# Attention, MoE and soft MoE on one core: where the sums of the attention weights are inverted

## The chip, the cores and the metric

The kernel runs on one core of a Trainium2 chip. A core has a matrix engine (TensorE, PE; its weight loads are listed as PEld), a vector engine (VectorE, DVE), a scalar engine (ScalarE, ACT), GpSimd (POOL) and a queue that issues transfers (SyncE, SP). The metric is the time of one execution on the device, in microseconds, as the median of several runs.

## The reference

```python
scores = (1 / sqrt(64)) * q @ k.T            # 4 batches, 12 heads, 448 rows, head size 64
scores = where(upper triangle, -1e9, scores)
attn = exp(scores - max(scores, axis=-1))
attn = attn / (attn.sum(axis=-1) + 1e-9)
x = (attn @ v), heads side by side           # 1792 x 768
g = leaky_relu(x @ w_in); x = g @ w_out      # 768 -> 2048 -> 768
logits = x @ phi                             # 32 slots: 8 experts of 4
slots = softmax over rows(logits).T @ x      # each expert: relu(. @ w1[e]) @ w2[e]
out = softmax over slots(logits) @ slot_out  # 1792 x 768
```

What matters here is the fourth line: every row of `attn @ v` is divided by the sum of the exponentials of its row.

## The kernel before, in words

Attention works on 24 pairs of heads (pair n is pair n % 6 of batch n // 6), transposed: keys lie on partitions in blocks of 112, the 448 query rows on columns. Pair n takes three slots of work. In slot A `attend` multiplies the exponentials of pair n - 1 with v (tile `O`, both heads, 64 partitions each), `lowering` brings the negated row maxima of pair n to columns, the product S3 and the product T0 of scores follow. In slot B `inverses(n - 1)` makes the row sums, then come S02 and T1. In slot C `columns(n - 1)` normalises, then come T2, S1 and the transposes `qkps` of a later pair. S tiles feed the row maxima (`junk`, line 361, on VectorE), T tiles the exponentials (`P`, line 397, on ScalarE). S and T tiles share two PSUM buffers, the many small products two buffers named "tr".

GpSimd masks the diagonal blocks of `P` and adds the key blocks into `tsum`, so that a row sum is a sum over partitions of `tsum` (and, for the first 112 rows, of the first block of `P`); partitions 112 to 127 hold small constants that add the reference's epsilon.

`inverses` (line 427): the weights `sixteen[:, i]` have ones in 16 of 64 columns and zeros in the others. Four products per head, accumulated in one tile `dn` of 128x112, place the sum of row 112 i + c into partitions 16 i to 16 i + 15 of column c. One reciprocal on VectorE (line 438) inverts all. `columns` (line 440): eight products with `first`, which picks one partition of r, spread the inverses to `rb`, 128x448, so that all 64 partitions of a head hold the inverse of their column. ScalarE copies that to SBUF (`rs`, line 452), VectorE multiplies with `O` and a scale (line 458), ScalarE rounds to fp16 (line 459) and GpSimd forms the remainder (line 460).

Each matrix product of type fp32 is two instructions in the trace, so eight products are 16.

From the second batch on, each slot also holds one of the 16 up products H of the batch before: 18 products of fp16 pieces (line 596) into one PSUM buffer, read by ScalarE (`g`, line 614) and then VectorE (line 615); the next H waits for that. Two of 18 slots in each batch have no H. Beside it, w_in is converted from 64 bit numbers during pairs 6 to 11, w_out after that: `cv`, `cs`, `w_am`, `w_m` (lines 108 to 245) on ScalarE, VectorE and GpSimd, and `wt_ps`, `wp_ps`, `wf_ps` (small products of w_out and phi) on TensorE. After attention comes the last up product with transposes `gps`, logits `L` and slot sums `pg`, then the experts, fed by a stream of w1 and w2 (line 820), whose buffers come free as TensorE finishes with what lies in them.

The order on each engine is set by the framework's list scheduler, which walks the program with its own costs and takes attention and H ahead of the conversions. Products made by `mm` and `tr` keep their program order on TensorE.

Of the kernel before, what the change touches and what calls it, by code (L numbers as in the profile page):

```python
# [10 lines left out]
F32 = mybir.dt.float32  # L11
# [23 lines left out]
def tile_attn_moe_softmoe(ctx: ExitStack, tc: tile.TileContext, q, k, v, w_in, w_out, phi, w1, w2, out, dbg=None):  # L35
    nc = tc.nc
    dbg = dbg or {}

    B, H, S, D = q.shape
# [5 lines left out]
    CP = 112  # L45
    NI = S // CP
    NP = H // 2
# [31 lines left out]
    att = tc.alloc_tile_pool(name="att", bufs=1, side="right")  # L79
# [9 lines left out]
    def ps_tr(name, shape=(128, 512)):  # L89
        return psum.tile(list(shape), F32, tag="tr", bufs=TR[0], name=name)  # L90
# [12 lines left out]
    mm = partial(in_order, nc.tensor.matmul)  # L103
# [310 lines left out]
    r_t = {}  # L414
# [11 lines left out]

    def inverses(n):

        p = pbuf[n % 2]
        dn = ps_tr(f"dn{n}", (128, CP))  # L430
        for i in range(NI):
            for a in range(2):
                x = p[0][:, a, 0, :CP] if i == 0 else tsum[:, a, CP * (i - 1) : CP * i]
                mm(
                    dn[64 * a : 64 * a + 64], sixteen[:, i], x, start=i == 0, stop=i == NI - 1, skip_group_check=True,
                )
        r_t[n] = r = att.tile([128, CP], F32, tag="r", bufs=1, name=f"r{n}")
        nc.vector.reciprocal(r, dn)

    def columns(n):  # L440

        b, hp = divmod(n, NP)
        o, r = o_t.pop(n), r_t.pop(n)
        rb = ps_tr(f"rb{n}", (128, S))
        for i in range(NI):
            for a in range(2):
                mm(
                    rb[64 * a : 64 * a + 64, CP * i : CP * (i + 1)], first[:, i, a], r, start=True, stop=True,
                    skip_group_check=True,
                )  # L450
        rs = att.tile([128, S], F32, tag="rs", bufs=1, name=f"rs{n}")
        nc.scalar.copy(rs, rb)
        if hp == 0:
            x16[b] = xpool.tile([128, CHUNK // 2], F16, tag="x16", name=f"x16_{b}")[:, : NP * 2 * S].rearrange(
                "p (c x s) -> p c x s", c=NP, x=2
            )
        hi = x16[b][:, hp, 0]
        nc.vector.scalar_tensor_tensor(rs, o, s_v[b], rs, ALU.mult, ALU.mult)
        nc.scalar.copy(hi, rs)  # L459
        nc.gpsimd.tensor_tensor(x16[b][:, hp, 1], rs, hi, ALU.subtract)  # L460

    NPAIR = B * NP
    onesr = att.tile([128, CP], F32R, name="onesr")
# [8 lines left out]
    first = att.tile([128, NI, 2, 64], F32, name="first")  # L472
# [12 lines left out]
    tsum = att.tile([128, 2, S - CP], F32, name="tsum")  # L485
# [6 lines left out]
    def attention_slots():  # L492
# [10 lines left out]
        for n in range(NPAIR + 1):  # L503
# [10 lines left out]
            if n > 0:  # L514
                inverses(n - 1)
# [5 lines left out]
            if n > 0:  # L521
                columns(n - 1)
# [226 lines left out]
    if True:  # L749
# [105 lines left out]
        for c in range(4):  # L855
            wo = loaded.pop(("wo", c))
            for h in range(2):
                for t in range(4):
                    nc.tensor.matmul(
                        psi[h][32 * t : 32 * t + 32], gdt[:, t, c], wo[:, t, 384 * h : 384 * (h + 1)],  # L860
                        start=c == 0, stop=c == 3, skip_group_check=True,
# [17 lines left out]
        for e in range(E):  # L879
            ph = ps2(f"ph{e}", (128, 256), tag="h", bufs=4)  # L880
            for hf in range(2):
                wt = loaded.pop(("w1", (e, hf)))
                for t in range(3):
                    for g in range(4):
                        nc.tensor.matmul(  # L885
                            ph[32 * g : 32 * g + 32], sit[:, 3 * hf + t], wt[:, t, 256 * g : 256 * (g + 1)],
                            start=hf == 0 and t == 0, stop=hf == 1 and t == 2, skip_group_check=True,
# [69 lines left out]
        for x, (t0, nt, c0, cols) in enumerate(pieces):  # L957
# [4 lines left out]
            for h in (0, 1) if cols == DM else (c0 // DH,):  # L962
                for t in range(nt):
# [3 lines left out]
                        start=t0 + t < 4, stop=t0 + t >= 8 * E - 4, skip_group_check=True,  # L967
# [52 lines left out]
```

## Time and profile before

| | us |
|---|---|
| median of 3 runs (lowest, highest) | 733.87 (732.2, 735.56) |
| the profiled execution | 740.27 |
| its span | 738.5 |
| TensorE busy | 639.2 |
| VectorE busy | 344.6 |
| ScalarE busy | 305.9 |
| GpSimd busy | 228.9 |

The span is the time from the first to the last instruction of the profiled execution, and busy times are sums over all stretches of the program. Pairs 0 to 5 are normalised in the first 105 us; pairs 6 to 23, which the change touches, between 121.9 and 505 us.

### The profile page before, as it was taken

How to read it: one execution, taken by the hardware profiler on the slowest of the kernel's cores; microseconds unless marked ns; L12 is line 12 of the kernel's file. 1: busy time of each engine (PE TensorE's matmuls, PEld its weight loads, DVE VectorE, ACT ScalarE, POOL GpSimd, SP SyncE). 2: the span in 40 equal slices, each digit the busy share in tenths (PEclk: the TensorE clock that was granted, in tenths of full speed). 3: DMA queues.
4: the chain of work that ended last, by engine and by line, in shares of the span. 5: the costliest groups of instructions: out<-in, count | busy, mean ns of one | idle time of the engine just before them, and what ended most of it. 6: DMA issues, size and time to landing. Idle time of an engine off the chain costs nothing.

```text
span 738.5 us, 13147 instructions
## 1 busy us (share of the span) xinstructions
PE 639.2 (87%) x5196; PEld 372.0 (50%) x5196; DVE 344.6 (47%) x923; ACT 305.9 (41%) x615; POOL 228.9 (31%) x247
## 2 busy tenths in 40 slices
PE   3888769999898999899999989999999997984573
PEld 2555445555555556566555555664656543541122
DVE  5887655666864544453354544324444433110013
ACT  1777543756774455444345454422322220110013
POOL 4577832656873332441223332320000000000000
PEclk9999968999999999899999999999999999999867
DMA  9933263455544454421153222014859247999988
GB/s 195 249 81 76 62 186 93 122 145 148 152 145 157 124 174 141 136 93 51 51 145 90 66 65 66 22 51 171 300 224 338 87 172 297 409 399 401 392 276 261
DMA packets 117709, 125.73 MB, mean 170 GB/s; under 512 B 69520, under 2 KB 99216, under 8 KB 117648
## 3 DMA queue, kind: packets, MB, share of 16 engines
q1 hardware_dynamic: 117648, 124.90, 52.6%
q8 instruction: 41, 0.67, 0.4%
q14 instruction: 20, 0.16, 0.1%
HBM read 105.74 MB, written 19.14 MB: 169 GB/s over the span
## 4 chain that ended last, share of the span: by engine, by line
PE 59%; DMA 15%; ACT 8%; DVE 7%; POOL 4%; issue 4%; SPq 2%; DVEq 0%; ACTq 0%; POOLq 0%
PE H L100 25%; DMA w<-in_moe_w_dram 7%; PE O L100 7%; PE gps L100 4%; PE T L100 4%; DMA v<-in_v_dram 3%; PE pg L100 2%; PE ph L885 2%; PE L L100 2%; DMA raw_i_None<-in_moe_w_in_dram 2%; PE qkps L100 2%; ACT mr L373 2%; PE dn L100 2%; PE rb L100 2%; DMA raw_o<-in_moe_w_out_dram 2%
## 5 line engine op out<-in xcount | busy, mean ns | idle before, releaser
L100 PE MATMUL H<-x,w 128*128 128x448 f16 x1152 | 244.4, 358 | 6.0 <-DVE g L615 6.0
L100 PEld LDWEIGHTS <-w 128*128 128x128 f16 x1152 | 110.1, 99 | 110.4 <-issue 29.7
L361 DVE CUSTOM_DVE_ANT_0 junk<-S,mask 112x448 bf16<-112x448 f32 (+1 forms) x192 | 84.9, 442 | 36.0 <-PE S L100 32.7
L615 DVE SCALAR_TENSOR_TENSOR g<-H,iv,g 128x448 f32<-128x448 f32 x58 | 39.6, 683 | 98.4 <-ACT g L614 96.0
L614 ACT ACTIVATE g<-H,iv 128x448 f32<-128x448 f32 x58 | 36.6, 631 | 81.2 <-PE H L100 70.9
L397 ACT ACTIVATE P<-T 112x672 f32<-112x672 f32 (+1 forms) x72 | 56.8, 788 | 32.3 <-PE T L100 32.3
L100 PE MATMUL O<-P,v 112*64 112x448 f32 (+3 forms) x384 | 59.2, 453 | 5.8 <-POOL P L401 4.6
L100 PE MATMUL T<-qkt 64*112 64x336 f32 (+3 forms) x576 | 58.7, 315 | 5.2 <-ACT P L397 4.5
L401 POOL TENSOR_SCALAR_AFFINE_SELECT P<-P 112x448 f32<-112x448 f32 x48 | 29.4, 613 | 99.9 <-ACT P L397 99.9
L965 PE MATMUL po<-w,hz 128*32 128x384 f32 x256 | 30.8, 608 | 24.9 <-DMA w<-in_moe_w_dram 24.9
L100 PEld LDWEIGHTS T<-qkt 64*112 64x112 f32 x576 | 44.8, 183 | 11.5 <-ACT P L397 5.8
L100 PEld LDWEIGHTS O<-P,v 112*64 112x64 f32 x384 | 27.9, 151 | 36.6 <-issue 16.9
L373 ACT ACTIVATE mr<-mps,own 128x112 fp32r<-128x112 f32 x96 | 26.1, 355 | 45.4 <-PE mps L100 45.4
L410 POOL TENSOR_TENSOR tsum<-tsum,P 112x448 f32<-112x448 f32 (+1 forms) x48 | 43.9, 915 | 2.7
L406 POOL TENSOR_TENSOR tsum<-P 112x672 f32<-112x672 f32 x24 | 40.7, 1694 | 1.7
L554 ACT COPY g_nat<-gps 112x512 f32<-112x512 f32 x32 | 18.7, 584 | 53.5 <-PE gps L100 53.5
L556 DVE COPY g_nat<-gps 112x512 f32<-112x512 f32 x32 | 22.1, 692 | 37.8 <-PE gps L100 37.5
L460 POOL TENSOR_TENSOR x<-rs,x 128x448 f16<-128x448 f32 x24 | 25.3, 1054 | 46.1 <-ACT x L459 46.1
L339 DVE TENSOR_TENSOR qkt<-qkps,qkt 128x448 fp32r<-128x448 f32 x48 | 28.3, 620 | 21.9 <-ACT qkt L338 21.8
L216 POOL TENSOR_TENSOR cv_i_None<-cv_i_None,cs_i_None 128x768 f32<-128x768 f32 x16 | 26.8, 1682 | 34.1 <-ACT cs_i_None L215 34.0
L100 PE MATMUL S<-qkt 64*112 64x448 f32 (+1 forms) x192 | 33.2, 387 | 3.6 <-DVE mxe L361 2.8
L100 PE MATMUL T<-mr,onesr 64*112 64x448 f32 (+1 forms) x192 | 32.1, 331 | 4.2 <-ACT mr L373 4.2
(178 smaller groups left out, 936.5 us busy)
## 6 DMA issues: line engine op xcount, KB each, us to landing
w<-in_moe_w_dram SPq DMA_DIRECT2D x32, 1536.0 KB, 18.2
raw_i_None<-in_moe_w_in_dram SPq DMA_DIRECT2D x16, 768.0 KB, 6.0
raw_o_None<-in_moe_w_out_dram SPq DMA_DIRECT2D x10, 768.0 KB, 5.1
g_far<-g SPq DMA_DIRECT2D x32, 224.0 KB, 2.0
gb<-g_far SPq DMA_DIRECT2D x8, 896.0 KB, 7.7
wo<-wsc SPq DMA_DIRECT2D x4, 1536.0 KB, 6.8
qk<-in_q_dram SPq DMA_DIRECT2D x48, 112.0 KB, 2.8
qk<-in_k_dram SPq DMA_DIRECT2D x48, 112.0 KB, 2.8
```

The source lines that it names most:

```text
L100: op(*args, **kwargs)
L216: nc.gpsimd.tensor_tensor(t, t, sg, ALU.mult)
L339: nc.vector.tensor_tensor(st[:, j, 1], p, st[:, j, 0].bitcast(F32), ALU.subtract)
L361: nc.vector.tensor_tensor_reduce(out=junk[:, :w], in0=ps[:, a, at : at + w], in1=mask[:, S - w :], scale=-1.0, scalar=3e38, op0=ALU.add, o ...
L373: nc.scalar.activation(mr[:, i], ps, AF.Copy, scale=own[:, i : i + 1])
L397: nc.scalar.activation(x[:, :, o : o + at], ps[:, :, :at], AF.Exp, scale=SCALE)
L401: nc.gpsimd.affine_select(out=d, in_=d, compare_op=ALU.is_ge, fill=0.0, base=0, pattern=[[0, 4], [1, CP]], channel_multiplier=-1,)
L406: nc.gpsimd.tensor_tensor(tsum[:CP], p[0][:CP, :, 0, CP:], p[0][:CP, :, 1, : S - CP], ALU.add)
L410: nc.gpsimd.tensor_tensor(y, y, p[1][:CP, :, j, : S - CP * (j + 2)], ALU.add)
L614: nc.scalar.activation(g, ps, AF.Copy, scale=iv[b][:, 0, f : f + 1])
L615: nc.vector.scalar_tensor_tensor(g, ps, iv[b][:, 1, f : f + 1], g, ALU.mult, ALU.max)
L965: nc.tensor.matmul(po[h][32 * g : 32 * g + 32], hp[:, (t0 + t) % 8], wt[:, t, DH * h - c0 : DH * (h + 1) - c0], start=t0 + t < 4, stop=t0 ...
```

## The change

For pairs 6 to 23 `inverses` uses weights of all ones (64 columns of `onesr`, read as fp32), so that every one of the 64 partitions of a head gets the sum of its column: two products per head, of 112 columns (first block) and of 336 (`tsum`), into `dn` of 128x448. ScalarE copies `dn` to `rs` at once, and VectorE inverts `rs` in place in two halves of 224 columns. `columns` then multiplies with `rs` directly; the products `rb` and the copy after them are gone. Pairs 0 to 5 are as before.

```diff
     def inverses(n):
         p = pbuf[n % 2]
+        if n >= NP:
+            dn = ps_tr(f"dn{n}", (128, S))
+            for c, x in ((slice(0, CP), p[0][:, :, 0, :CP]), (slice(CP, S), tsum)):
+                for a in range(2):
+                    mm(dn[64 * a : 64 * a + 64, c], onesr[:, :64].bitcast(F32), x[:, a], start=True, stop=True, skip_group_check=True)
+            r_t[n] = rs = att.tile([128, S], F32, tag="rs", bufs=1, name=f"rs{n}")
+            nc.scalar.copy(rs, dn)
+            for c in range(0, S, S // 2):
+                nc.vector.reciprocal(rs[:, c : c + S // 2], rs[:, c : c + S // 2])
+            return
         dn = ps_tr(f"dn{n}", (128, CP))
...
         o, r = o_t.pop(n), r_t.pop(n)
-        rb = ps_tr(f"rb{n}", (128, S))
...
-        rs = att.tile([128, S], F32, tag="rs", bufs=1, name=f"rs{n}")
-        nc.scalar.copy(rs, rb)
+        if n < NP:
+            rb = ps_tr(f"rb{n}", (128, S))
...
+            rs = att.tile([128, S], F32, tag="rs", bufs=1, name=f"rs{n}")
+            nc.scalar.copy(rs, rb)
+        else:
+            rs = r
```

The scheduler places the rest anew. On TensorE, slot C of the 17th pair (pair 16) before; wf_ps and wt_ps are the preparation of w_out, T_2 and S_1 the products T2 and S1:

```order
L100 MATMUL wf_ps_3989<-istack,w_7_3920 128x32
L100 MATMUL wt_ps_0_3993<-ident,cv_o_None 128x128 x3
L100 MATMUL wt_ps_1_3998<-ident,cv_o_None 128x128 x3
L100 MATMUL rb_4003<-r_3939,first 64x112 x8
L100 MATMUL T_2_4017<-qkt_3533 112x224 x6
L100 MATMUL T_2_4017<-mr_3865,onesr 112x224 x2
L100 MATMUL T_2_4017<-qkt_3533 112x112 x6
L100 MATMUL T_2_4017<-mr_3865,onesr 112x112 x2
L100 MATMUL S_1_4038<-qkt_3777 112x224 x2
```

and the same place now:

```order
L100 MATMUL wf_ps_3857<-istack,w_7_3790 128x32
L100 MATMUL wt_ps_0_3861<-ident,cv_o_None 128x128 x3
L100 MATMUL wt_ps_1_3866<-ident,cv_o_None 128x128 x3
L100 MATMUL T_2_3874<-qkt_3416 112x224 x6
L100 MATMUL T_2_3874<-mr_3735,onesr 112x224 x2
L100 MATMUL T_2_3874<-qkt_3416 112x112 x6
L100 MATMUL T_2_3874<-mr_3735,onesr 112x112 x2
L100 MATMUL S_1_3895<-qkt_3647 112x224 x2
```

Only rb is gone; the preparation stands where it stood. On VectorE, slot B of the same pair before (ISA rows are the maxima; each is followed by a short row that writes its result):

```order
L438 RECIPROCAL r_3939<-dn_3930 128x112
L361 ISA junk_0_0_3946,mxe_143<-S_0_3941,mask 112x112
L361 ISA mxe_143 112x1
L361 ISA junk_0_1_3948,mxe_143<-S_0_3941,mask 112x112
L361 ISA mxe_143 112x1
L361 ISA junk_2_0_3950,mxe_143<-S_0_3941,mask 112x336
L361 ISA mxe_143 112x1
L361 ISA junk_2_1_3952,mxe_143<-S_0_3941,mask 112x336
L361 ISA mxe_143 112x1
L615 SCALAR_TENSOR_TENSOR g_12_3985<-H_12_3966,iv_2837,g_12_3985 128x448
L458 SCALAR_TENSOR_TENSOR rs_4012<-O_3854,v_s,rs_4012 128x448
```

and now:

```order
L361 ISA junk_0_0_3814,mxe_143<-S_0_3809,mask 112x112
L361 ISA mxe_143 112x1
L439 RECIPROCAL rs_3805<-rs_3805 128x224 x2
L361 ISA junk_0_1_3816,mxe_143<-S_0_3809,mask 112x112
L361 ISA mxe_143 112x1
L472 SCALAR_TENSOR_TENSOR rs_3805<-O_3724,v_s,rs_3805 128x448
L361 ISA junk_2_0_3818,mxe_143<-S_0_3809,mask 112x336
L361 ISA mxe_143 112x1
L361 ISA junk_2_1_3820,mxe_143<-S_0_3809,mask 112x336
L361 ISA mxe_143 112x1
L629 SCALAR_TENSOR_TENSOR g_12_3853<-H_12_3834,iv_2759,g_12_3853 128x448
```

The product with O has moved ahead of two maxima and of g, and the two reciprocals stand ahead of three of the four maxima. On VectorE, slot B of the 10th pair (pair 9), from the reciprocal to g, before; w_m, w_am and cv_i belong to the conversion of w_in:

```order
L438 RECIPROCAL r_2196<-dn_2187 128x112
L615 SCALAR_TENSOR_TENSOR g_8_2159<-H_8_2140,iv_1378,g_8_2159 128x448
L361 ISA junk_0_0_2203,mxe_144<-S_0_2198,mask 112x112
...
L361 ISA junk_2_1_2209,mxe_144<-S_0_2198,mask 112x336
L361 ISA mxe_144 112x1
L116 TENSOR_SCALAR w_e<-w_m_2250 128x1
L118 TENSOR_SCALAR w_s<-w_e 128x1
L121 TENSOR_SCALAR inv_w<-w_e 128x1
L199 TENSOR_REDUCE w_am_2352<-cv_i_None 128x1
L200 TENSOR_SCALAR cv_i_None<-cv_i_None 128x768
L615 SCALAR_TENSOR_TENSOR g_9_2244<-H_9_2225,iv_1378,g_9_2244 128x448
```

and now, from the reciprocals on (g_8 stands ahead of them):

```order
L439 RECIPROCAL rs_2153<-rs_2153 128x224 x2
L361 ISA junk_0_1_2164,mxe_144<-S_0_2157,mask 112x112
L361 ISA mxe_144 112x1
L113 TENSOR_REDUCE w_m_2209<-w_ps 128x1
L472 SCALAR_TENSOR_TENSOR rs_2153<-O_2066,v_s,rs_2153 128x448
...
L199 TENSOR_REDUCE w_am_2300<-cv_i_None 128x1
L361 ISA junk_2_1_2168,mxe_144<-S_0_2157,mask 112x336
L361 ISA mxe_144 112x1
L116 TENSOR_SCALAR w_e<-w_m_2209 128x1
L199 TENSOR_REDUCE w_am_2382<-cv_i_None 128x1
L200 TENSOR_SCALAR cv_i_None<-cv_i_None 128x768
L629 SCALAR_TENSOR_TENSOR g_9_2203<-H_9_2184,iv_1378,g_9_2203 128x448
```

A second reduction and the product with O stand ahead of g_9 now, and a reduction stands ahead of the last maximum.

## Rows read from the trace of the kernel before

**Rows 1.** The page's first part: busy time of each engine, share of the span.

```profile
PE 639.2 (87%) x5196; PEld 372.0 (50%) x5196; DVE 344.6 (47%) x923; ACT 305.9 (41%) x615; POOL 228.9 (31%) x247
```

**Rows 2.** Busy time by stretch: stretch, length, busy (instructions), granted clock, DMA.

```profile
121.90:230.70 108.80, 101.17 (x760) 58.83 (x759) 74.26 (x200) 71.42 (x133) 67.35 (x53) 0.95 0.50 145
247.20:380.50 133.30, 127.74 (x1075) 78.71 (x1074) 60.29 (x161) 64.44 (x137) 44.63 (x43) 0.97 0.35 107
380.50:505.00 124.50, 115.99 (x966) 71.25 (x966) 54.31 (x129) 55.15 (x119) 38.65 (x42) 0.99 0.22 63
183.60:207.60 24.00, 21.98 (x156) 12.27 (x155) 19.08 (x46) 17.61 (x33) 17.22 (x13) 0.93 0.53 157
```

**Rows 3.** The waits of SyncE's queue: total us, times, longest.

```profile
SPq L820 <- PE H L100: 42.2, 4, 20.7
```

**Rows 4.** Instructions on rb, rs and dn, 121 to 505 us: min/median/max ns.

```profile
L100 PE MATMUL rb<-r,first x288: 259/259/311, 127.8 to 502.5; 128*64 128x112 f32 x144
L452 ACT COPY rs<-rb x18: 509/533/547, 129.7 to 502.8; 128x448 f32<-128x448 f32 x18
...
L438 DVE RECIPROCAL r<-dn x18: 841/850/858, 123.3 to 497.7; 128x112 f32<-128x112 f32 x18
```

**Rows 5.** Timeline of TensorE in pair 16: start, length, instruction.

```profile
340.74 0.41 PE L100 MATMUL dn<-P,sixteen 128*64 128x112 f32 x4
...
341.66 0.51 PE L100 MATMUL S<-qkt 64*112 64x112 f32 x4
...
346.13 0.31 PE L100 MATMUL wf_ps<-istack,w 96*128 96x32 f32 x2
...
347.57 0.99 PE L100 MATMUL rb<-r,first 128*64 128x112 f32 x16
...
348.49 0.56 PE L100 MATMUL T<-qkt 64*112 64x224 f32 x6
...
349.34 0.31 PE L100 MATMUL S<-qkt 64*112 64x224 f32 x2
```

**Rows 6.** Timeline of TensorE, the attend product and its successor.

```profile
332.44 2.11 PE L100 MATMUL O<-P,v 112*64 112x448 f32 x16
334.48 0.32 PE L100 MATMUL mps<-ident,mxe 112*128 112x112 f32 x1
```

**Rows 7.** Timeline of VectorE in pair 16; idle time before in brackets.

```profile
341.78 0.86 DVE L438 RECIPROCAL r<-dn 128x112 f32<-128x112 f32 x1 [0.44 <-PE dn L100]
342.55 0.21 DVE L361 CUSTOM_DVE_ANT_0 junk<-S,mask 112x112 bf16<-112x112 f32 x1
...
343.67 0.51 DVE L361 CUSTOM_DVE_ANT_0 junk<-S,mask 112x336 bf16<-112x336 f32 x1
...
347.00 0.68 DVE L615 SCALAR_TENSOR_TENSOR g<-H,iv,g 128x448 f32<-128x448 f32 x1 [2.82 <-ACT g L614]
...
349.23 0.68 DVE L458 SCALAR_TENSOR_TENSOR rs<-O,v_s,rs 128x448 f32<-128x448 f32 x1 [1.55 <-ACT rs L452]
```

**Rows 8.** VectorE's instructions with source and destination in SBUF: min/median/max ns.

```profile
L698 DVE RECIPROCAL cs<-cs x4: 177/177/178, 510.1 to 615.5; 112x4 f32<-112x4 f32 x4
...
L200 DVE TENSOR_SCALAR cv_i_None<-cv_i_None x16: 498/555/2658, 21.9 to 197.3; 128x768 int32<-128x768 int32 x16
...
L199 DVE TENSOR_REDUCE w_am<-cv_i_None x16: 940/945/954, 20.9 to 195.6; 128x1 f32<-128x768 f32 x16
```

**Rows 9.** Timeline of TensorE and VectorE in pair 9.

```profile
186.66 3.56 PE L100 MATMUL H<-x,w 128*128 128x448 f16 x18 [0.55 <-DVE g L615]
...
191.92 0.31 PE L100 MATMUL S<-qkt 64*112 64x224 f32 x2
...
194.84 5.25 PE L100 MATMUL H<-x,w 128*128 128x448 f16 x18 [0.90 <-DVE g L615]
...
191.54 2.66 DVE L200 TENSOR_SCALAR cv_i_None<-cv_i_None 128x768 int32<-128x768 int32 x1
194.12 0.67 DVE L615 SCALAR_TENSOR_TENSOR g<-H,iv,g 128x448 f32<-128x448 f32 x1
```

More of the change, by code (lines that the diff above doesn't have):

```diff
@@ L443, in columns @@
         o, r = o_t.pop(n), r_t.pop(n)
-        rb = ps_tr(f"rb{n}", (128, S))
[L445 to L450, printed above, removed]
-        rs = att.tile([128, S], F32, tag="rs", bufs=1, name=f"rs{n}")
-        nc.scalar.copy(rs, rb)
+        if n < NP:
+            rb = ps_tr(f"rb{n}", (128, S))
+            for i in range(NI):
+                for a in range(2):
+                    mm(
+                        rb[64 * a : 64 * a + 64, CP * i : CP * (i + 1)], first[:, i, a], r, start=True, stop=True,
+                        skip_group_check=True,
+                    )
+            rs = att.tile([128, S], F32, tag="rs", bufs=1, name=f"rs{n}")
+            nc.scalar.copy(rs, rb)
+        else:
+            rs = r
         if hp == 0:
```

## The prediction

> **What bounds the kernel now.** I read the page's first part, then busy time by stretch, then the rows of what the change touches, then the order of instructions in single slots. The page says TensorE 87% of the span, VectorE 47% [rows 1]. By stretch the picture is sharper [rows 2]: while pairs 6 to 11 are normalised (121.9 to 230.7 us) TensorE is busy 93% of the time and VectorE 68%; for pairs 12 to 17 it is 96% and 45%, for pairs 18 to 23 93% and 44%. So TensorE sets the pace wherever the change acts, and VectorE has slack, least in the first of the three stretches. The end of the kernel is a weight stream, but its loads wait for TensorE to free their slots: SyncE waits on the last up products alone for 42.2 us [rows 3]. A gain before 505 us therefore moves the loads along too, and I carry it to the end in full.
>
> **What goes.** For the 18 pairs 6 to 23 the eight products `rb` go, 16 instructions each (x288 in all) [rows 4]. In pair 16 they hold TensorE from 347.57 to 348.49, 0.92 us, and nothing hides them: the next product follows at once, and the span before them is full [rows 5]. 18 x 0.92 = 16.6 us.
>
> **What is replaced.** `dn` held TensorE from 340.74 to 341.66, 0.92 us, with eight products of 112 columns [rows 5]. The new one streams as many columns (2 x 112 + 2 x 336 = 896) in four products. No row shows this shape. The nearest is the attend product: 64-column weights of the same type, 2,240 columns in 332.44 to 334.48, 2.04 us [rows 6], so 0.91 ns a column and 0.82 us for 896. Bounds: 0.92 (only the columns count) and 0.75 (a little less than the attend rate). I take 0.83, that is 0.09 saved, 18 x 0.09 = 1.6 us. The sums still wait for the same `tsum` on GpSimd. Gross gain on TensorE: 18.2 us, 1.01 a pair.
>
> **What is added.** ScalarE's copy of 128x448 (0.53 us [rows 4]) exists before and after; it moves one slot earlier, in front of the exp of T1, which waits for later products anyway. I cost it at nothing on ScalarE; but it now stands between `dn` and the reciprocals. VectorE's one reciprocal of 128x112 (0.85 us [rows 4]) becomes two of 128x224, SBUF to SBUF. That shape is not in the trace. Two rows bracket it: 112 elements from PSUM take 0.85 us, 4 elements from SBUF 0.177 us [rows 4, 8]; the slope is (850 - 177) / 108 = 6.23 ns an element, which gives 0.85 + 112 x 6.23 ns = 1.55 us for 224. Bounds: 0.85 (two elements at a time, since the source is now SBUF) and 1.70 (twice the row). I take 1.55, as the longer row and the short one lie on it. VectorE gains 2 x 1.55 - 0.85 = 2.25 us a pair, 40 us over 18 pairs; by the averages above it has room, so the question is whether the wait lands on TensorE.
>
> Two things on TensorE hang on VectorE in a slot. The next H product needs `g` (H has one buffer), and S1 (in pairs 7 and some others T2) needs the buffer of S02, free only when VectorE has made its four maxima (`junk`). Before, the reciprocal stood ahead of these and all was done 2.8 us before `g` [rows 7].
>
> **A plain slot, pair 16.** Let t = 0 be the end of `dn` (341.66). TensorE: S02, T1 and H follow, and the next product starts at +4.47 (346.13); then preparation p (1.44 us here: 346.13 to 347.57), then T2, and S1 is reached 0.85 after T2 starts [rows 5], so at +5.32 + p. VectorE: copy of ScalarE done at about +0.7, two reciprocals 2 x 1.47 (an instruction starts 0.08 before the last one's end: 0.86 long, next at +0.77 [rows 7]) to +3.65; one short maximum, whose partner can go before, 0.33; `rs` 0.68 long, 0.60 to the next; two maxima of 336, 0.51 and a short row, 0.58 each [rows 7]: +5.75, and with the signal about +5.85. `g` then runs when H is done. S1 stalls for 5.85 - 5.32 - p = 0.53 - p. With p = 1.44 the 1.01 us is kept whole; with p = 0 half of it goes.
>
> **The other slots.** The order of instructions gives p and what else stands ahead of the last maximum.
> - Pairs 12 to 17: 12 has no preparation there (0.5 lost), 17 only a short one (0.3). In 13 to 15 a conversion of 0.9 us and `g` stand ahead of the last maximum, with a longer p; about 0.3 each. Lost 1.7, kept 6 x 1.01 - 1.7 = 4.4.
> - Pairs 18 to 23: 18 starts late behind four conversions (0.9); the others have preparation and a transposed piece inside H, and 22 and 23 have no maxima left. Kept 5.2.
> - Pairs 6 to 11: here VectorE also converts w_in. Pair 9 is the worst. Reciprocals from 186.6 to 189.5; maxima, a small reduction and `rs`, 1.7 us; a reduction of 0.95 [rows 8]; the last maximum, 0.6: done at about 192.7, against S1 at 191.92 before [rows 9]. Another reduction and the conversion stand ahead of `g`, which comes at 195 to 196.5, against 194.12. So pair 9 loses 1.5 net. Pair 10 (conversions between the maxima) loses 1.3, pair 6 0.3; pairs 7, 8 and 11 keep 0.8, 1.0 and 0.5 (in 7 the reciprocals stand behind all maxima). Sum of the six: -0.8.
>
> Sum: 4.4 + 5.2 - 0.8 = 8.8 us. The profiled execution took 740.27 us (span 738.5), so 731.5 by its own time; it lies 6.4 us above the median of the runs, 733.87, and I put the gain on the median: 725.1.
>
> [...] The row that decides is the reciprocal's. A TENSOR_SCALAR of 768 elements, SBUF to SBUF, takes 0.5 us where a TENSOR_REDUCE of as many takes 0.945 [rows 8]: some instructions do take two elements at a time. [...] The 4-element row (177 ns) is too short to tell.
>
> **The rivals.**
> - *Two elements at a time.* Each reciprocal 0.85 us, 1.4 us less a pair. For it: source and destination are in SBUF, and the 0.5 us row. Against: the 4-element row lies on the line of one at a time. The stalls of pairs 12 to 23 vanish and those of 6, 9 and 10 shrink by 1.4: gain 18.2 - 3 = 15.2, 718.7 us. GpSimd might then be held up: the 2.66 us that a 0.5 us conversion took at 191.54 [rows 8, 9] shows the two engines in each other's way.
> - *The gain is given back.* VectorE is 0.5 us later a slot than I count, in all slots (`rs`, qkt and the conversions come later and hold S1, `g` or the next slot's transposes). For it: the margin in a plain slot is p, and ScalarE's copy is queued behind 0.9 us conversions in places. Against: 2.8 us of idle VectorE ahead of `g` [rows 7]. 18 x 0.5 more lost: no change, 734.
> - *VectorE becomes the bound in pairs 6 to 11: slower.* In pair 9's stretch it is busy 19.08 of 24.0 us [rows 2]; 2.25 + 0.53 (the copy in its chain) leaves 2. Where conversions keep it from getting ahead, each of the six pairs pays 2.8 instead of gaining. [...] 6 x 2.8 + two such drops 3.4 - 9.6 kept later = 10.6 slower, 744; it decides once `g` is later than TensorE's other work of the slot by over 1.5 us in most of the six pairs.
> - *It doesn't do what it says*: the 336-column products could cost more than eight short ones. The attend rows speak against it; it would stay within the second rival.
>
> **How the numbers follow.** Forecast 0.47 (its own range 721 to 730); two at a time 0.15; given back 0.23; slower 0.15. Range for 8 in 10: 716 to 737, from the second case's neighbourhood to just above no change, leaving out most of the slower case. What this measurement can tell from no change is 0.5%, 3.7 us, so 730.2 to 737.5 is "same". Faster: 0.47 + 0.15, less a little for a forecast that falls short, plus a little of the given-back case: 0.62. Same 0.23. Slower 0.15.
>
> **What will show it.** `rb` from the 7th pair on absent, `dn` 0.83 us in eight instructions; the two reciprocals at 1.55 us each; H of pair 16 following as before, TensorE's waits for `junk` in S rows some 0.5 us and only where no preparation stands; in pairs 9 and 10 waits of 1 to 2 us; TensorE's idle time before 230 us up by 5 to 7 us. Reciprocals near 0.85 or 1.7 us, lower clock in 120 to 230 us, or waits of S or H over 1 us in pairs 12 to 23 would make the prediction wrong.

## Result and profile after

| | before | after |
|---|---|---|
| median of the runs timed together, us | 733.41 | 724.51 |
| ratio of the comparison, 95% interval | | 0.985 (0.981 to 0.989) |
| a later comparison, more runs | | 0.9905 (0.987 to 0.994) |
| profiled execution's span, us | 738.5 | 720.6 |

One execution after took 1462.87 us, twice the others; the ratio leaves it out, while the median of 724.51 counts it (without it 722.34). The change makes the kernel 7 to 11 us faster; the prediction was 8.8 us and 725.1. The two profiled executions lie 17.9 us apart, which is more than the change is worth: both kernels scatter by several us from one execution to the next, and the first trace of before was a long one, that of after a short one. So below several traces of each are set side by side.

The page's first part after, to be held against [rows 1]:

```profile
PE 615.5 (85%) x4764; PEld 348.7 (48%) x4764; DVE 378.6 (53%) x941; ACT 304.7 (42%) x615; POOL 232.1 (32%) x247
```

VectorE has 34 us more, 432 matrix instructions are gone. What the touched tiles take now (min/median/max ns), against [rows 4]:

```profile
L100 PE MATMUL dn<-P,onesr x72: 259/284/311, 120.8 to 479.4; 128*64 128x112 f32 x72
...
L100 PE MATMUL dn<-tsum,onesr x72: 446/446/446, 121.0 to 479.8; 128*64 128x336 f32 x72
...
L437 ACT COPY rs<-dn x18: 505/534/537, 121.8 to 480.3; 128x448 f32<-128x448 f32 x18
...
L439 DVE RECIPROCAL rs<-rs x36: 1490/1520/1554, 122.4 to 482.4; 128x224 f32<-128x224 f32 x36
```

The products `rb` are gone from pair 6 on, and a reciprocal takes 1.52 us, forecast 1.55. Pair 16 on TensorE, from `dn` to S1, to be read beside [rows 5] (start, length, instruction, idle time before it):

```profile
331.86 0.41 PE L100 MATMUL dn<-P,onesr 128*64 128x112 f32 x4
332.10 0.73 PE L100 MATMUL dn<-tsum,onesr 128*64 128x336 f32 x4
332.76 0.50 PE L100 MATMUL S<-qkt 64*112 64x112 f32 x4
...
337.24 0.31 PE L100 MATMUL wf_ps<-istack,w 96*128 96x32 f32 x2
...
338.47 0.55 PE L100 MATMUL wt_ps<-ident,cv_o_None 128*128 128x128 f32 x3 [0.56 <-ACT wprime L258]
...
339.80 0.31 PE L100 MATMUL S<-qkt 64*112 64x224 f32 x2
```

`dn` holds TensorE for 0.90 us (331.86 to 332.76), against 0.92 before. S1 is reached 7.04 us after `dn`'s end and doesn't wait. VectorE and ScalarE in the same pair, to be read beside [rows 7]:

```profile
333.51 2.96 DVE L439 RECIPROCAL rs<-rs 128x224 f32<-128x224 f32 x2
...
336.52 0.68 DVE L472 SCALAR_TENSOR_TENSOR rs<-O,v_s,rs 128x448 f32<-128x448 f32 x1
...
338.09 0.08 DVE L361 DVE_READ_ACCUMULATOR2_ANT mxe<- 112x1 f32 x1
...
337.24 0.57 ACT L473 CAST x<-rs 128x448 f16<-128x448 f32 x1 [2.57 <-DVE rs L472]
337.71 0.63 ACT L628 ACTIVATE g<-H,iv 128x448 f32<-128x448 f32 x1
```

The last maximum is done at 338.17, 5.4 us after `dn` and well ahead of S1 at 339.80. But ScalarE's rounding (`x`) now stands ahead of `g` in its queue and waits for VectorE's `rs`. `g` starts only behind it, at 337.71, and behind `g` stand the copies that the preparation on TensorE waits for: 0.56 us at 338.47. Both traces of before have 0.30 at this place (the prediction counted it in its p of 1.44); in the first:

```profile
347.10 0.55 PE L100 MATMUL wt_ps<-ident,cv_o_None 128*128 128x128 f32 x3 [0.30 <-ACT wprime L258]
```

**By stretches.** TensorE's `dn` marks the start of each pair's work, so a stretch from `dn` of pair 6 to that of pair 12 is the same work in every kernel. Pairs whose code is unchanged in an experiment count as before, changed ones as after; the traces are the first two and those of the experiments below (in this order: as before the first two, then `late` and `late2`, or `first6`; as after the first two, then `first6`, or `late` and `late2`). The start up to pair 6 isn't listed; its code is unchanged.

| stretch, us | as before | as after | forecast gain | gain of the means |
|---|---|---|---|---|
| pairs 6 to 11 | 125.2, 123.6, 124.7, 125.3 | 121.4, 129.0, 131.6 | -0.8 | -2.7 |
| pairs 12 to 17 | 133.3, 132.0, 130.8 | 127.4, 127.4, 128.3, 127.2 | 4.4 | 4.5 |
| pairs 18 to 22 and the start of 23 | 116.0, 113.6, 116.8 | 109.7, 107.9, 108.4, 107.7 | 5.2 (to the end of 23) | 7.0 |
| from there to the end | 242.0, 240.7, 239.2 | 241.4, 241.7, 242.9, 242.6 | 0 | -1.5 |

These means give 7.4 us in all, inside what the comparisons say. The -2.7 is the least certain: its three traces after lie 10 us apart. Of the 17.9 us between the first two traces 3.8 lie in pairs 6 to 11, where 121.4 is a value that no other trace of this code reached, 5.9 and 6.3 in the two stretches behind, where the first trace of before is longer than the second (133.3 and 132.0, 116.0 and 113.6), 0.7 at the end and 1.2 ahead of pair 6.

### The profile page after: what moved, and what is told of

The parts are those of the page before. It is cut to its first block, busy times and chain, and to the rows that moved or that the text cites. A ratio compares the mean times of both kernels' runs of the same rounds, so it can differ in the third digit from the quotient of the medians.

```text
span 720.6 us, 12298 instructions
## 1 busy us (share of the span) xinstructions
PE 615.5 (85%) x4764; PEld 348.7 (48%) x4764; DVE 378.6 (53%) x941; ACT 304.7 (42%) x615; POOL 232.1 (32%) x247
## 4 chain that ended last, share of the span: by engine, by line
PE 51%; DMA 14%; DVE 14%; ACT 9%; POOL 4%; issue 4%; SPq 2%; DVEq 0%; ACTq 0%; POOLq 0%
PE H L100 22%; DMA w<-in_moe_w_dram 8%; PE O L100 6%; PE gps L100 4%; DVE rs L439 3%; DMA v<-in_v_dram 3%; DVE junk L361 2%; DMA raw_o<-in_moe_w_out_dram 2%; PE pg L100 2%; PE ph L899 2%; PE T L100 2%; PE L L100 2%; ACT mr L373 2%; DMA raw_i_None<-in_moe_w_in_dram 2%; ACT g L628 2%
## 5 line engine op out<-in xcount | busy, mean ns | idle before, releaser
L100 PE MATMUL H<-x,w 128*128 128x448 f16 x1152 | 240.9, 354 | 7.3 <-DVE g L629 6.1
L100 PE MATMUL O<-P,v 112*64 112x448 f32 (+3 forms) x384 | 56.9, 439 | 6.4 <-POOL P L401 6.0
L439 DVE RECIPROCAL rs<-rs 128x224 f32<-128x224 f32 x36 | 53.3, 1522 | 1.6 <-ACT rs L437 1.6
L979 PE MATMUL po<-w,hz 128*32 128x384 f32 x256 | 29.0, 575 | 25.2 <-DMA w<-in_moe_w_dram 25.2
L410 POOL TENSOR_TENSOR tsum<-tsum,P 112x448 f32<-112x448 f32 (+1 forms) x48 | 45.9, 956 | 2.8
```

Source lines behind the costliest of these rows:

```text
L100: op(*args, **kwargs)
L410: nc.gpsimd.tensor_tensor(y, y, p[1][:CP, :, j, : S - CP * (j + 2)], ALU.add)
L439: nc.vector.reciprocal(rs[:, c : c + S // 2], rs[:, c : c + S // 2])
L979: nc.tensor.matmul(po[h][32 * g : 32 * g + 32], hp[:, (t0 + t) % 8], wt[:, t, DH * h - c0 : DH * (h + 1) - c0], start=t0 + t < 4, stop=t0 ...
```

## The experiments

Ratios are against the kernel before on the same chip, with 95% intervals.

**Both kernels again.** No edit.

> The kernel before, unchanged, once more. It gives a second trace of it and the scatter of the comparison. If the profiled execution that the prediction read (740.3 us) was a late one by chance, this trace's span lies near 731 to 735 us and the ratio to the kernel before is 1.000 +- 0.004. If it was typical of a profiled execution, the span is again near 738. TensorE's lower clock level, 24 us of it between 100 and 500 us in the first trace, tells which stretches scatter.

Ratio 1.0015 (0.998 to 1.005), span 734.9: the first trace was a long one. (Its lower clock level, a granted clock of 0.50, takes 34 us between 100 and 500 us, a mean granted clock of 0.96, and not 24; 24 of them lie before 230 us.)

> The changed kernel, unchanged, once more. Prediction's account: a gain of 8.8 us, ratio 0.988, 18 times 1.01 less 9.4 us of lateness of VectorE. Rival account, read from the first trace after: rb's 0.92 us a pair is kept nearly whole (18 x 0.92 = 16.6 us less 1 to 2 us of waits), ratio 0.979 to 0.981.

Ratio 0.9905 (0.987 to 0.994), span 729.4. So the first trace of before was 3.6 us above the second, and the forecast's account fits better than the rival that the first trace after suggested. The scatter sits in pairs 6 to 11. That stretch in the first trace after (stretch, length, TensorE busy and instructions, its weight loads, VectorE, ScalarE, GpSimd, granted clock, DMA):

```profile
120.76:242.19 121.43, 108.97 (x749) 60.65 (x749) 93.95 (x234) 78.92 (x149) 74.40 (x59) 0.99 0.49 146
```

and in the second:

```profile
123.36:252.39 129.03, 113.48 (x749) 61.95 (x749) 97.02 (x234) 79.08 (x149) 74.09 (x59) 0.95 0.47 138
```

The same 749 instructions are busy 4.5 us longer at a mean granted clock of 0.95 instead of 0.99 (in the first trace it is 0.50 for 3.4 us, from 192.20 to 195.61, and 1.00 in the rest of the stretch), and TensorE idles 15.5 instead of 12.5 us.

**The two halves of the change.** `late` applies it to pairs 12 to 23, `first6` to pairs 6 to 11.

```diff
-        if n >= NP:
+        if n >= 2 * NP:        # late
+        if NP <= n < 2 * NP:   # first6
...
```

The condition in `columns` follows.

> The change for pairs 12 to 23 alone; pairs 6 to 11 as before. Prediction's account: the first six changed pairs lose 0.8 us, so without them the gain is 9.6 us, ratio 0.987, a little better than the whole change. Rival account (every pair keeps nearly its rb): 12 of 18 pairs, two thirds of the whole gain; 10 us if the whole is 15, 7 us if the whole is 11.

> The change for pairs 6 to 11 alone; pairs 12 to 23 as before. Prediction's account: 0.8 us slower than before, ratio 1.001. Rival account (each pair keeps nearly its rb of 0.92 us): 4 to 5 us faster, ratio 0.994.

`late` 0.989 (0.985 to 0.993), `first6` 1.005 (1.002 to 1.008): the gain is made in pairs 12 to 23, and pairs 6 to 11 alone make the kernel 3.7 us slower. The sign is the forecast's, the size is more than its 0.8. `late` once more:

> The change for pairs 12 to 23 alone, once more, to place it against the whole change. By the traces pairs 6 to 11 cost the whole change 2.9 us on the mean of three (127.4 against 124.5), so this should be 724 to 727, ratio 0.986, and the whole change 0.988 to 0.990. Rival: they don't differ, ratio 0.989 or 0.990.

0.987 (0.984 to 0.991). With 0.985 and 0.9905 for the whole change the two can't be told apart: these comparisons don't show the loss of `first6` in the whole change. `first6` in the stretch of pairs 6 to 11, same columns as above:

```profile
121.99:253.63 131.64, 114.98 (x749) 63.42 (x748) 94.78 (x234) 78.83 (x149) 73.56 (x59) 0.94 0.46 135
```

16.7 us idle and the lowest clock of the three: waits and clock together took 10 us more than in the first trace after. The second trace of before has 9.3 us idle and a clock of 0.99:

```profile
125.03:248.58 123.55, 114.23 (x894) 68.11 (x893) 83.84 (x228) 78.89 (x149) 73.93 (x59) 0.99 0.50 144
```

**The products put back.**

```diff
         else:
             rs = r
+            rb = ps_tr(f"rb{n}", (128, S))
+            for i in range(NI):
+                for a in range(2):
+                    mm(rb[64 * a : 64 * a + 64, CP * i : CP * (i + 1)], first[:, i, a], onesr.bitcast(F32), ...)
```

> The changed kernel with eight products as rb's put back in their old place in pairs 6 to 23, into a tile that nobody reads (they take ones in place of r, so that they wait for nothing). If rb's time on TensorE is what was gained, 0.92 us a pair comes back in pairs 12 to 23: 11 us, ratio 1.005 to 1.008, slower than before, since VectorE's burden stays; in pairs 6 to 11 less than 5.5 us comes back, as TensorE waits there anyway. Rival: the gain comes from the product with O moved ahead or from the earlier copy; the time then stays near 727, ratio 0.990.

1.001 (0.999 to 1.004): the whole gain is gone, and with it the rival, whose two causes are still in this kernel. Pair 16 shows where it went:

```profile
344.21 0.55 PE L100 MATMUL wt_ps<-ident,cv_o_None 128*128 128x128 f32 x3 [0.56 <-ACT wprime L258]
344.69 0.99 PE L100 MATMUL rb<-onesr,first 128*64 128x112 f32 x16
345.61 0.57 PE L100 MATMUL T<-qkt 64*112 64x224 f32 x6
```

The pair takes 23.27 us from its `dn` to the next, 22.34 without: 0.93 for rb's 0.92, at an unchanged wait of 0.56 us. In that pair the gain is TensorE's time. The stretches don't add up as well: pairs 12 to 17 take 130.9 and 18 to 22 115.9 us, 3.3 and 7.5 more than the means after, where rb alone would be 5.5 and 4.6. Other waits moved too (`rb` itself waits 0.70 us in pairs 14 and 15, for ScalarE's copy `wt`). Pairs 6 to 11 take 125.0 us, no more than after: as far as one trace says, TensorE's work isn't what sets the time there.

**VectorE's load, less and more.** `norecip` leaves the reciprocals out:

```diff
-            for c in range(0, S, S // 2):
-                nc.vector.reciprocal(rs[:, c : c + S // 2], rs[:, c : c + S // 2])
```

> The changed kernel without the two reciprocals (the sums are copied to rs and not inverted, and the last product of pairs 6 to 23 takes a minimum and a maximum instead of two factors). TensorE's work stays that of the changed kernel; VectorE has 3.0 us a pair less. If VectorE's lateness is what eats the gain in pairs 6 to 11, their stretch (from the sums of pair 6 to those of pair 12) falls from 127 to 131 us to about 119 (124.5 before less 5.6), pairs 12 to 23 win another 1 to 2 us by the waits of S1, and the whole is 718 to 720, ratio 0.978. Rival: the loss comes from the new order of instructions or the copy on ScalarE; then the stretch stays at 127 to 131 and the ratio at 0.989 to 0.991.

0.990 (0.986 to 0.994), 724.1 us span: no better than the changed kernel; the forecast of 718 to 720 failed. Pairs 12 to 17 take 127.4 us (after: 127.4), 18 to 22 105.8 (108.4), 6 to 11 130.0. In pair 16 the rounding comes 3 us ahead of `g`, which now waits for H alone, as the ScalarE rows show:

```profile
344.67 0.56 ACT L471 CAST x<-rs 128x448 f16<-128x448 f32 x1 [0.76 <-DVE rs L470]
...
347.89 0.63 ACT L626 ACTIVATE g<-H,iv 128x448 f32<-128x448 f32 x1 [2.02 <-PE H L100]
```

The pair takes 22.09 us and keeps 0.92, all of rb. Elsewhere in pairs 12 to 17 other waits for ScalarE fill the place (1.21 us in pair 13 and 0.83 in pair 14, for copies of the preparation). In pairs 6 to 11 no S waits for the maxima any more (none over 0.2 us), but H waits for `g`, 3.2 us in pair 7 and 5.7 in pair 9, whose timeline shows why:

```profile
194.60 3.65 DVE L200 TENSOR_SCALAR cv_i_None<-cv_i_None 128x768 int32<-128x768 int32 x1
198.29 1.22 DVE L201 SCALAR_TENSOR_TENSOR cv_i_None<-raw_i_None,cv_i_None 128x768 int32<-128x768 int32 x1
...
200.60 0.67 DVE L627 SCALAR_TENSOR_TENSOR g<-H,iv,g 128x448 f32<-128x448 f32 x1
...
193.62 1.63 POOL L406 TENSOR_TENSOR tsum<-P 112x672 f32<-112x672 f32 x1
195.21 1.04 POOL L472 TENSOR_TENSOR x<-rs,x 128x448 f16<-128x448 f32 x1
196.20 1.64 POOL L216 TENSOR_TENSOR cv_i_None<-cv_i_None,cs_i_None 128x768 f32<-128x768 f32 x1
197.79 0.91 POOL L401 TENSOR_SCALAR_AFFINE_SELECT P<-P 112x448 f32<-112x448 f32 x1
...
201.32 6.04 PE L100 MATMUL H<-x,w 128*128 128x448 f16 x18 [5.68 <-DVE g L627]
```

A conversion that takes 0.555 us by its median [rows 8] takes 3.65 us, as three GpSimd products run back to back beside it, and ends 0.41 us after the last of them (198.25 and 197.84). `g` stands behind it, H waits 5.68 us, and then takes 6.04 us instead of 3.56, at a mean granted clock of 0.58.

`recipmore` inverts the first half of `rs` three times:

```diff
-            for c in range(0, S, S // 2):
+            for c in (0, 0, 0, S // 2):
```

> The changed kernel with the first half of rs inverted three times in each of pairs 6 to 23: 2 x 1.5 = 3.0 us more on VectorE a pair, ahead of the last maxima. In the trace after, the last maximum of S02 of pair 16 is done 5.4 us after dn's end and S1 is reached at 7.0, so 1.3 to 1.5 us of wait arise there; if VectorE's margin is as small as that everywhere, 12 x 1.5 in pairs 12 to 23 and 6 x 3 in pairs 6 to 11, 36 us in all: 763, ratio 1.037. Rival: VectorE is off the path in pairs 12 to 23 (45% busy), only pairs 6 to 11 pay: 745, ratio 1.013.

1.0475 (1.043 to 1.053), 768.3 us, near the 763 of the forecast and far from the rival. The three stretches take 139.2, 138.8 and 120.1 us, each 11 to 12 more than the means after (the forecast had 18 and, for the two later ones together, 18). Three us less on VectorE a pair win 0.2 in pairs 12 to 17, three us more lose 11: the change uses up about the slack that was there.

**Without ScalarE's copy.**

```diff
-            nc.scalar.copy(rs, dn)
-                nc.vector.reciprocal(rs[:, c : c + S // 2], rs[:, c : c + S // 2])
+                nc.vector.reciprocal(rs[:, c : c + S // 2], dn[:, c : c + S // 2])
```

> The changed kernel with the reciprocals reading dn in PSUM and writing rs, without ScalarE's copy. If a reciprocal's time goes by its elements alone, they stay at 1.5 to 1.6 us; they begin some 0.6 us earlier, so the last maximum of each slot is done 0.6 us earlier: 2 to 4 us gained in pairs 6 to 11, up to 1 us behind that, 723, ratio 0.985. Rival: dn's buffer, one of two for the small products, is held 2.4 us longer, and preparation and transposes wait for it: 730 or more, ratio 0.993.

1.0085 (1.005 to 1.012), slower than before. The reciprocal itself costs the same from PSUM:

```profile
L438 DVE RECIPROCAL rs<-dn x36: 1487/1518/1558, 122.9 to 501.8; 128x224 f32<-128x224 f32 x36
```

Pairs 12 to 17 are as after (127.9), 6 to 11 take 134.2 and 18 to 22 115.5. In pair 19 the transposes wait 1.25 us for a copy of ScalarE (`wt`) out of one of the small buffers. That isn't the hold of `dn`: `dn` is read by 411.06, and the copy stands in the queue behind a conversion that waits 1.31 us for its load:

```profile
415.52 0.54 ACT L197 ACTIVATE cs_o<-raw_o 128x384 bf16<-128x384 f32 x1 [1.31 <-DMA raw_o<-in_moe_w_out_dram]
415.97 0.46 ACT L245 COPY wt<-wt_ps 128x384 f32<-128x384 f32 x1
```

In pairs 7 to 9 the waits are H's, for `g`, 2.8 to 4.3 us each. How much the longer hold of `dn` and how much the other order has of that stays open.

**The conversions left out.** Both kernels without the integer instructions of lines 200 and 201:

```diff
-        nc.vector.tensor_scalar(ti, ti, 3, None, ALU.logical_shift_left)
-        nc.vector.scalar_tensor_tensor(ti, lw, 29, ti, ALU.logical_shift_right, ALU.bitwise_or)
```

> The kernel before without the two integer instructions of each conversion on VectorE (lines 200 and 201; the weights then have wrong values of a like size). It is the base for the next run. VectorE has 16 us less work in pairs 6 to 11, 22 to 23 by the time that these instructions took there. If they hold up g, whose lateness cost TensorE 4 to 5 us there, the stretch from the sums of pair 6 to those of pair 12 falls from 124.5 to 118 to 121 us, and the time by 4 to 8 us, ratio 0.990 to 0.995. Rival: what waits there waits for ScalarE and GpSimd, and nothing changes: 1.000.

0.994 (0.991 to 0.997), pairs 6 to 11 in 118.6 us:

```profile
125.14:243.78 118.64, 114.12 (x893) 67.00 (x893) 63.52 (x206) 78.37 (x149) 70.40 (x59) 0.99 0.51 150
```

> The changed kernel without the same two instructions. If it is these conversions, stretched beside GpSimd, that turn the gain of pairs 6 to 11 into a loss, the change is worth in that stretch what it saves on TensorE, 5 to 6 us against the run before (113 to 116 us), and 15 to 17 us in all. Rival, the three us of reciprocals alone suffice: then the stretch is no shorter than in the run before, and the change is worth 8 to 11 us in all, as with the conversions.

0.976 (0.972 to 0.979). The change is now worth 0.0184 x 735.2 = 13.5 us, by the two intervals some 10 to 17: more than the 7 of the comparison with more runs, not clearly more than the 11 of the first, and not clearly less than the 15 to 17 of the theory. Its pairs 6 to 11:

```profile
123.80:240.45 116.65, 108.81 (x750) 60.97 (x749) 74.75 (x212) 78.81 (x149) 70.69 (x59) 0.99 0.52 152
```

Here the change wins 2.0 us by one trace each (118.6 to 116.7), where it loses 2.7 with the conversions, but not the 5 to 6 of the theory. Most of the extra lies elsewhere: in pairs 12 to 17 these two traces differ by 8.1 us (132.2 to 124.1) instead of 4.5, for the edit takes the same instructions out of the conversion of w_out too. So the conversions seem to have a part in the loss of pairs 6 to 11; how much of it is theirs and how much the reciprocals' stays open, since leaving out the reciprocals alone won nothing there either.

## Why the prediction was right

- **TensorE bounds, and a gain there goes to the end.** Right for pairs 12 to 23: putting the products back takes the gain back (1.001). For pairs 6 to 11 TensorE's busy share of 93% misled: with rb's work put back there the stretch is no longer than without, by one trace. To the end, 1.5 us of 8.9 are missing behind pair 23's start; the three and four traces overlap there (239.2 to 242.0 and 241.4 to 242.9), so that stays open.
- **rb, 0.92 us a pair.** Right: 0.93 in pair 16 by the products put back.
- **dn, 0.09 saved.** Mis-sized: 0.02 (0.92 to 0.90). The rate of the attend product doesn't carry over to products of 112 and 336 columns; of the bounds given, the upper one holds. That is 1.3 us of the sum.
- **The reciprocal, 1.55 us.** 1.52, from SBUF and from PSUM alike. The rival of two elements at a time, 0.85 us, the author's estimate beside the 0.5 us row [rows 8], falls.
- **A plain slot.** Right in S1, which doesn't stall in pair 16, wrong in what the pair keeps: 1.01 forecast, 0.67 measured (23.01 to 22.34). In the second trace after, the waits of S for the maxima in pairs 14 and 15 are 0.22 us each, near the forecast's 0.3; pair 12, forecast at 0.5, has none. What took 0.26 us of pair 16's gain is ScalarE's rounding ahead of `g` in the queue, which the prediction had left out: it had costed ScalarE at nothing. That the six pairs together came to the forecast is luck in part: pair 16 kept less, pairs 12 and 17 more (0.83 and 1.35 by the second traces, against 0.5 and 0.7).
- **Pairs 12 to 17: 4.4 forecast, 4.5 measured. Pairs 18 to 23: 5.2 forecast, 7.0 measured up to the start of 23.** In the second part the excess over rb's five times 0.92 goes with waits that shrank: in pairs 19 and 20 TensorE waited 1.0 us for `g_nat` and 1.7 for `qkt`, and in the second trace after 0.4 and 0.9. In pair 21 a wait for `l` grew from 0.4 to 1.3, and the pair kept nothing (23.57 to 23.53). By the second traces alone the gain there is 5.7, so part of the 7.0 is scatter.
- **Pairs 6 to 11: -0.8 forecast, -2.7 measured.** The sign was right, and so were some of its signs: TensorE's idle time in the stretch rose from 8.9 to 14.9 us on the means (5 to 7 more foretold), and S1 waits for the maxima 0.8 to 0.9 us in pair 9 and 1.1 to 2.6 in pair 10. The prices of the pairs were not: 9, called the worst, won 0.7 on the means, since its waits of before went, while 6 lost 1.3, 7 lost 0.9 and 11 lost 2.2. In pair 6, put at 0.3, S1 waits 0.89 us for ScalarE's `P` and T 0.9 for its `mr` in all three traces after and in none of before. What the third rival fears, a late `g`, shows too, and so does a lower clock, above all in the second trace after and in `first6` (a mean granted clock of 0.95 and 0.94 in the stretch); the three executions differ by 10 us. Its term of 3.4 us for two drops no run shows as a cost of the change: in the stretch the first trace of before has three H at 5.25 us or a little more instead of 3.56 (at 166.94, 194.84 and 225.49), the first after has one (5.18 at 192.30), and in the second after TensorE is busy 4.5 us longer than in the first. The rival doesn't decide the whole, since pairs 12 to 23 win more. Waits of pairs 6 and 10 in the first trace after:

```profile
128.44 0.36 PE L100 MATMUL S<-qkt 64*112 64x224 f32 x2 [0.89 <-ACT P L397]
138.25 0.46 PE L100 MATMUL T<-mr,onesr 64*112 64x448 f32 x2 [0.89 <-ACT mr L373]
212.88 0.36 PE L100 MATMUL S<-qkt 64*112 64x224 f32 x2 [1.07 <-DVE mxe L361]
```

The total came out right by luck in part, because errors offset each other: pairs 6 to 11 were put 1.9 us too high, 18 to 23 1.8 too low, and behind them 1.5 are missing. Two of the prediction's signs of being wrong are there without making it wrong: a wait of H over 1 us in pair 18 of the first trace after (1.12), which before has as well (1.19), and a lower clock in pairs 6 to 11 of the second (0.95, before 0.96 and 0.99).

## What to carry to other kernels

Work may be traded from a busy engine to an idle one as long as the idle time lies where the work goes: 2.2 us more on VectorE a slot (2 x 1.52 - 0.85) cost little in pairs 12 to 23, the next three cost some 40 over the kernel (0.9905 to 1.0475). Ask of every queue, not only of the two engines traded between, what now waits at its head. And where a stretch scatters by more than the gain, as pairs 6 to 11 do here, don't read the gain off one trace: take several.

## What the hardware showed

- The reciprocal's time goes by its elements here: 0.85 us for 112 of each partition (from PSUM) and 1.52 for 224 (from PSUM and from SBUF), 6.0 ns an element between the two.
- A VectorE integer operation of 0.555 us (line 200) took up to 2.66 in the first trace of before [rows 8] and up to 3.65 in `norecip` while GpSimd products ran beside it; another, SCALAR_TENSOR_TENSOR on two SBUF tiles (line 201), 0.95 by its median and up to 3.18 (`psum`). With no GpSimd product beside them, none took over 0.57 and 0.97 us on 768 elements, in eleven traces. Reciprocals beside the same products stayed at 1.49 to 1.56. The 3.65 us lie beside three GpSimd products, of 1.04 to 1.64 us each. GpSimd took longer too: its addition of line 406, 1.61 us by its median in the first trace of before, took 2.20 to 2.22 in the three cases where line 201 was running as it began (40.33, 108.30 and 213.35).
- TensorE's granted clock has two values in the first traces of before and after, 1.00 and 0.50, and 0.50 came after some of its waits: in the first trace of before it held from 195.14 to 198.56, after the wait of 0.90 us that ended at 194.84. After the four longest waits of H seen in pairs 6 to 11 (3.2 to 5.7 us, in `norecip` and `psum`) the 18 products of H took 5.9 to 6.4 us instead of 3.56, at a mean granted clock of 0.55 to 0.59; after waits of 0.9 to 3.1 us they took 3.56 in most cases, 5.0 to 5.3 in others and once 6.5 (`recipmore`). The same wait of 0.90 us in pair 9 was followed by 5.25 us in the first trace of before and by 3.56 in `late`.
